# Second MLP of an attention and two-MLP kernel: weight sums and low parts on VectorE, tied to later steps

## The chip, the cores and the metric

The kernel runs on one core of a Trainium2 chip. The metric is device time in microseconds (us) of one execution; the kernel before takes 1208.81 us, the median of three executions (1207.57 to 1208.98).

## The reference, cut to what matters

Windowed attention (4 batches, 8 heads, 768 positions, head size 64) gives x with 3072 tokens of 512 features. A first MLP makes y = (sigmoid(x Wg) * (x Wv)) Wo with 1536 hidden features. The second MLP, the stage of the change, is

```
h = y @ w_in                                  # 3072 x 512 times 512 x 2048
g = h * (1.0 / (1.0 + np.exp(-1.702 * h)))
out = g @ w_out                               # 2048 x 512
```

The weights come as 64-bit floats. Every product is computed in three matmuls on split operands: a high part (h) in the type fp32r and a low part (l), the rest of the value, as h*h + h*l + l*h.

## The kernel before, in words

All work is added as tasks to a list (`add`), each with an engine, an estimated duration, the keys that it reads and writes, and perhaps a due time. `Schedule.run` walks through time by these estimates: on each engine it starts the ready task with the earliest due time, and it never leaves an engine idle for a later, more urgent task. The order it finds is the order of the instructions on each engine's queue; on the chip each engine works its queue off in that order and waits where an operand is late. Products on TensorE get due times from a running clock (`clock`, advanced by `c_mm`), and all that feeds them gets due times from theirs.

The 3072 tokens are six blocks of 512. The second MLP takes blocks 0 and 1 plainly: 16 steps per block, f = 0 to 15, each `first_product` (12 matmuls: 8 "high", line 742, and 4 "low", line 749), then sigmoid on ScalarE (766), the multiplication on VectorE (769, tile sig), the high part on ScalarE (772, tile gh) and the low part (776, tile gl), then `gemm4` (12 matmuls, 720) for the step before, whose result stays in four banks over 16 steps. The low part of block 0 is made by GpSimd (POOL), that of block 1 by VectorE.

Blocks 2 and 3, and then 4 and 5, are taken as two pairs. For a pair the first product is done in a form with 7 products instead of 8 (m1 to m7 in `part_product`, line 1248, 6 matmuls each) on sums of quarter blocks. This needs two preparations.

- `combine(j)`, j = 0 to 7, forms sums of the weights of two slots: `whole` adds high and low part of a slot (1093, tiles cw_a and cw_b, on POOL), `sums` forms four combinations (1103 to 1106, tile cw_s, one task of four VectorE instructions), `high` (1109, ScalarE, tile cw_h) and two `low` (1113, VectorE, tile cw_l), and DMAs of SP store all to wc_dram. The tiles exist once, so one combine follows another. `fetch` loads the parts back into a ring (sb_r).
- `x_prep(b)` loads eight tiles of the blocks' y (1203), forms eight differences (1209, VectorE) and cuts fourteen operands into high (1188, ScalarE) and low part (1192; eight of the fourteen on POOL, six on VectorE).

All eight combines and the first x_prep are ready as soon as the weights are converted, in block 0. Within a pair, each j has the seven products of a group, gating on ScalarE and VectorE (1260, 1264, 1289, 1292, 1275, 1278), and one or two `gemm4` of hidden parts made earlier (`fill`). After j = 7 come 16 rounds of one `gemm4` and one `halves` (the high and low part of a stored g, 1275 and 1278); only then, in the order of the program, the second pair begins. The x_prep of the second pair stands ahead of these rounds; its loads depend on y alone.

Of the kernel before, what the change touches and what calls it, by code (L numbers as in the profile page):

```python
# [8 lines left out]
F32 = mybir.dt.float32  # L9
# [6 lines left out]
ALU = mybir.AluOpType  # L16
AX = mybir.AxisListType

P = 128
# [100 lines left out]
def c_dve(n, k=1):  # L120
    return k * 0.13 + n / 960.0
# [6 lines left out]
def c_pool(n):  # L128
    return 0.1 + n * 2.4e-3
# [3 lines left out]
def kernel(  # L133
# [14 lines left out]
    nc = tc.nc  # L148
# [7 lines left out]
    F2 = w2_in.shape[1] // P  # L156
# [7 lines left out]
    BLK = 512  # L164
# [8 lines left out]
    add = sch.add  # L173
# [540 lines left out]
    def mm3(ps_out, lhs, rhs, first, last):  # L714

        n = len(lhs)
        for i in range(n):
            (lh, ll), (rh, rl) = lhs[i], rhs[i]
            for j, (a, c) in enumerate(((lh, rh), (lh, rl), (ll, rh))):
# [5 lines left out]
                    stop=(last and i == n - 1 and j == 2),  # L725
                )

    def c_mm(n, k):
        return k * (n / 2400.0 + 0.0025)

    def product(dur, fn, r, w, load=1.0):
        add("pe", dur, fn, r=r, w=w, due=clock[0])
        clock[0] += dur * load
# [81 lines left out]
    for i in range(4):  # L815
        x = Bufs(pro, "", [], main)
# [177 lines left out]

    freed = []
    for f in range(F1):
        freed.append((3 * f + 1, f))
# [12 lines left out]
        convert(slot_in2[f], cols(w2_in, f))  # L1012
        convert(slot_out2[f], rows(w2_out, f))

    def gemm4(f, i, banks, row, end=False, after=()):

        gh, gl = ghs[i], gls[i]
        s = slot_out2[f]

        def fn():  # L1020
            w = slots[s]
            for tt in range(TT):
                c = slice(tt * P, (tt + 1) * P)
                mm3(bank[banks[tt]], [(gh[:, c], gl[:, c])], [(w[:, 0, :], w[:, 1, :])], f == 0, f == F2 - 1)

        product(
            c_mm(512, 3 * TT),
            fn,
            [("w", s, 0), ("w", s, 1), ("gh", i), ("gl", i), *after],
            [("bank", k) for k in banks],  # L1030
        )
        if f < F2 - 1:
            return
        for tt in range(TT):
            st, kst = (fts[tt], ("f", tt)) if end else stage()
            bk = banks[tt]
            h = 256 if end and tt == TT - 1 else 512
            for c in range(0, 512, h):

                def ev(on_dve, c=slice(c, c + h), st=st, bk=bk):  # L1040
                    if on_dve:
                        nc.vector.tensor_copy(st[:, c], bank[bk][:, c])
                    else:
                        nc.scalar.activation(st[:, c], bank[bk][:, c], AF.Copy)

                def store(tt=tt, c=slice(c, c + h), st=st):
                    r = row + tt * P
                    nc.sync.dma_start(out=out[r : r + P, c], in_=st[:, c])

                on_dve = bool(tt % 2) or c > 0  # L1050
                k = (kst, c) if h < 512 else kst
                add("dve" if on_dve else "act", c_dve(h), lambda ev=ev, d=on_dve: ev(d), r=[("bank", bk)], w=[k])
                add("sp", 0.45, store, r=[k], nbytes=P * h * 4)
# [33 lines left out]
    def combine(j):  # L1087
        s0, s1 = slot_in2[2 * j], slot_in2[2 * j + 1]

        def whole(x, s):  # L1090
            def fn():
                w = slots[s]
                nc.gpsimd.tensor_tensor(out=cw[x], in0=w[:, 0, :].bitcast(F32), in1=w[:, 1, :].bitcast(F32), op=ALU.add)

            add("pool", c_pool(512), fn, r=[("w", s, 0), ("w", s, 1)], w=["c" + x])

        whole("wa", s0)
        whole("wb", s1)

        def sums():  # L1100
            wa, wb, s = cw["wa"], cw["wb"], cw["s"]
            tt = nc.vector.tensor_tensor
            tt(out=s[:, 0, :], in0=wb[:, :H2], in1=wb[:, H2:], op=ALU.add)  # L1103
            tt(out=s[:, 2, :], in0=wa[:, :H2], in1=wb[:, :H2], op=ALU.subtract)  # L1104
            tt(out=s[:, 1, :], in0=s[:, 0, :], in1=wa[:, :H2], op=ALU.subtract)
            tt(out=s[:, 3, :], in0=wa[:, H2:], in1=s[:, 1, :], op=ALU.subtract)

        def high():
            nc.scalar.activation(cw["h"], cw["s"], AF.Copy)  # L1109

        def low(h):
            c = slice(2 * h, 2 * h + 2)
            nc.vector.tensor_tensor(  # L1113
                out=cw["l"][:, c, :], in0=cw["s"][:, c, :], in1=cw["h"][:, c, :].bitcast(F32), op=ALU.subtract
            )

        add("dve", c_dve(4 * H2, 4), sums, r=["cwa", "cwb"], w=["cws"])
        add("act", c_act(4 * H2), high, r=["cws"], w=["cwh"])
        for h in range(2):
            add("dve", c_dve(2 * H2), lambda h=h: low(h), r=["cws", "cwh"], w=["cwl"])  # L1120

        def put(m, n, part, src, keys):
            def fn():
                at = wc_dram[j * NMP + m : j * NMP + m + n]
                if part is None:
                    nc.sync.dma_start(out=at[0].rearrange("p (h k) -> p h k", h=2), in_=src())
                else:
                    nc.sync.dma_start(out=at[:, :, part * H2 : (part + 1) * H2].rearrange("c p k -> p c k"), in_=src())

            kw = [("wc", j, m + i, h) for i in range(n) for h in ((0, 1) if part is None else (part,))]  # L1130
            add("sp", 0.45, fn, r=keys, w=kw, nbytes=n * P * H2 * (8 if part is None else 4))

        for m, s, c in ((MA11, s0, 0), (MA12, s0, H2), (MA22, s1, H2)):
            put(m, 1, None, lambda s=s, c=c: slots[s][:, :, c : c + H2].bitcast(F32), [("w", s, 0), ("w", s, 1)])
        put(MS1, 4, 0, lambda: cw["h"].bitcast(F32), ["cwh"])
        put(MS1, 4, 1, lambda: cw["l"].bitcast(F32), ["cwl"])

    for j in range(NPR):
        combine(j)

    xt, ringh, gbs, work, ys = {}, {}, {}, {}, {}
    NRH = 14
# [51 lines left out]
        add("act", c_act(BLK), hi, r=[kst], w=[("X", m, k)])  # L1194
        add("pool" if pool else "dve", c_pool(BLK) if pool else c_dve(BLK), lo, r=[kst], w=[("X", m, k)])

    def x_prep(b):
        for k in range(2):
            tk = 4 + k
            for i, (m, bb) in enumerate(((k, b), (k, b + 1), (2 + k, b), (2 + k, b + 1))):  # L1200

                def load(i=i, m=m, bb=bb):
                    nc.sync.dma_start(out=ys[i], in_=y_dram[m * P : (m + 1) * P, bb * BLK : (bb + 1) * BLK])

                add("sp", 0.45, load, r=[("y", m, bb)], w=[KYS[i]], nbytes=P * BLK * 4)

            def sub(o, x, y):
                def fn():
                    nc.vector.tensor_tensor(out=ys[o], in0=ys[x], in1=ys[y], op=ALU.subtract)

                add("dve", c_dve(BLK), fn, r=[KYS[x], KYS[y]], w=[KYS[o]])

            def cut(m, i, pool):
                split_x(m, k, lambda: ys[i], KYS[i], pool)

            cut(XB11, 0, True)
            sub(tk, 1, 0)
            cut(XT1, tk, False)
            cut(XB21, 2, True)
            sub(tk, 3, tk)  # L1220
            cut(XT2, tk, False)
            cut(XB22, 3, True)
            sub(1, 3, 1)
            cut(XT3, 1, True)
            sub(tk, 2, tk)
            cut(XT4, tk, False)

# [8 lines left out]
            kr = [("wc", g % NPR, STEPS[m][0], x) for x in range(2)]  # L1236
            add("sp", 0.45, fn, r=kr, w=[("ring", h)], nbytes=P * 512 * 4)

    def part_product(g, m, bk, first):
        h = (g * NMP + SEQ.index(m)) % NRH  # L1240
        x = STEPS[m][1]

        def fn():
            w = ringh[h]
            for k in range(2):
                for wl, xl in ((0, 0), (0, 1), (1, 0)):
                    o = wl * H2 + k * P
                    nc.tensor.matmul(  # L1248
                        bank[bk],
                        w[:, o : o + P],  # L1250
                        xt[x, k][:, xl, :],
                        start=first and k == 0 and wl == 0 and xl == 0,
                        stop=k == 1 and wl == 1,
                        skip_group_check=not first,
                    )

        product(c_mm(512, 6), fn, [("ring", h)] + xkey(x), [("bank", bk)])

    def snap(n, bk):
        add("act", c_act(BLK), lambda: nc.scalar.activation(work[n], bank[bk], AF.Copy), r=[("bank", bk)], w=[n])  # L1260
# [23 lines left out]
    def gate2(src, ksrc, f=None):  # L1284
# [11 lines left out]
            return halves(lambda: sigs[i], ks)  # L1296
        add("dve", c_dve(BLK), mul, r=[ksrc, ks], w=[("gB", f)])

    pend = None
    nh = 0  # L1300
    for b in range(NBP):
        xb = (NB + b) % 2
        for f in range(F2):
            hb = Hb[nh % 2]
            nh += 1
            first_product(slot_in2[f], xb, BLK, hb)
            i, tail = gated(BLK, hb, 1.702, hb, b == 0)
            tail()
            if pend:
                gemm4(*pend)  # L1310
            if f == 0 and b + 1 < NBP:
                y_in(b + 1, (xb + 1) % 2)
            pend = (f, i, O[b], b * BLK)
# [5 lines left out]
    homes = [(m, k) for m in (XB21, XT2, XB22, XT3, XT4) for k in range(2)]  # L1319
    for (m, k), s in zip(homes, rest2 + slot_in2):  # L1320
        open_slot_as(s, f"sb_x{m}{k}", F32R, x_one(m, k), [("X", m, k)])
    x_prep(NBP)
    left = slot_in2[len(homes) - len(rest2) :]
    for i in range(NRH // 2):

# [18 lines left out]
    for sb in range(NSB):  # L1344
# [5 lines left out]
        for j in range(NPR):  # L1350
# [18 lines left out]
            gate2(lambda: work["s5"], "s5", 2 * j + 1)  # L1369
            if fill:  # L1370
                gemm4(*fill.pop(0))
            part_product(g, "m4", a, False)
            ic = gate2(lambda a=a: bank[a], ("bank", a))
            if g + 2 < NSB * NPR:
                fetch(g + 2)
            fill += [(2 * j, ia, oa, row), (2 * j + 1, ic, oa, row)]
        if sb + 1 < NSB:
            x_prep(NBP + 2 * sb + 2)
        end = sb == NSB - 1
        for f in range(F2):  # L1380
            gemm4(*fill.pop(0))
# [36 lines left out]
```

## Time and profile before

| What | Value |
|---|---|
| Median of three executions | 1208.81 us |
| The profiled execution | 1209.48 us, of which the span from first to last instruction is 1207.7 us |
| PE (TensorE matmul) busy | 1180.2 us, 98% of the span, 7352 instructions |
| DVE (VectorE) busy | 712.2 us, 59% |
| ACT (ScalarE) busy | 522.2 us, 43% |
| POOL (GpSimd) busy | 153.3 us, 13% |
| Chain of waits that ended last | 90% PE, 5% DVE, 2% ACT |

Matmuls overlap in the pipeline: a busy time of 390 ns per matmul is not its cost. The cost is the distance from the start of one matmul to the start of the next. In a row, "x4" merges four instructions, the time in front is the first one's start, and a bracket tells how long the engine stood idle before the row and what released it.

### The profile page before, as it was taken

The numbers are of one execution on the slowest core, as the hardware profiler recorded it, in microseconds if no ns is written. First come the engines' busy times: TensorE is split into PE (matmuls) and PEld (weight loads), VectorE is DVE, ScalarE is ACT, GpSimd is POOL, SyncE is SP. The second block draws the span as 40 slices with busy tenths as digits, with TensorE's granted clock in tenths as the row PEclk, the third lists the DMA queues.
The fourth block names the chain that finished last, engine by engine and source line by source line (L and its number), as shares of the span: only waits on it lengthen the run. The fifth ranks groups of instructions, "written<-read, shape, count | busy, mean of one in ns | idle before, by whom it ended". The sixth has DMA issues, their size and how long they took to land.

```text
span 1207.7 us, 19184 instructions
## 1 busy us (share of the span) xinstructions
PE 1180.2 (98%) x7352; PEld 982.2 (81%) x7352; DVE 712.2 (59%) x1406; ACT 522.2 (43%) x847; POOL 153.3 (13%) x128
## 2 busy tenths in 40 slices
PE   6799999999999999999999999999999999999998
PEld 5688799988888888888888877888888878888887
DVE  6898848884588438816778776252143374143342
ACT  4598743443344223413577643342243343243332
POOL 2221210000010000000211276320000030000000
PEclk9799999999999999999999999999999999999999
DMA  9556333233123202400477654032144443234100
GB/s 217 141 176 199 115 81 54 50 53 76 31 50 63 50 13 50 97 2 19 130 257 243 197 198 158 31 103 94 55 148 123 123 139 95 63 114 122 44 36 35
DMA packets 200780, 122.08 MB, mean 101 GB/s; under 512 B 138608, under 2 KB 173680, under 8 KB 200688
## 3 DMA queue, kind: packets, MB, share of 16 engines
q1 hardware_dynamic: 197232, 114.56, 35.0%
q10 hardware_dynamic: 3456, 6.29, 1.4%
q8 instruction: 58, 0.95, 0.3%
q14 instruction: 34, 0.28, 0.1%
HBM read 93.54 MB, written 27.26 MB: 100 GB/s over the span
## 4 chain that ended last, share of the span: by engine, by line
PE 90%; DVE 5%; ACT 2%; issue 1%; DMA 1%; POOL 0%; DVEq 0%; SPq 0%; ACTq 0%; POOLq 0%
PE bank L742 25%; PE bank L720 19%; PE bank L917 16%; PE bank L749 12%; PE bank L1248 12%; PE bank L656 2%; PE bank L506 2%; DVE cw_l L1113 1%; DVE cw_s L1103 1%; PE bank L596 1%; ACT cw_h L1109 0%; DVE pw L574 0%; PE bank L397 0%; DVE cw_s L1104 0%; PE bank L389 0%
## 5 line engine op out<-in xcount | busy, mean ns | idle before, releaser
L742 PE MATMUL bank<-xh,w 128*128 128x512 f32 (+1 forms) x784 | 284.7, 370 | 3.5 <-ACT w L286 1.6
L742 PE MATMUL bank<-xl,w 128*128 128x512 f32 (+1 forms) x784 | 282.9, 368 | 0.0
L720 PE MATMUL bank<-w,gh 128*128 128x512 f32 x768 | 237.7, 391 | 0.1
L749 PE MATMUL bank<-xh,w 128*128 128x512 f32 (+1 forms) x784 | 191.7, 370 | 0.0
L742 PEld LDWEIGHTS bank<-xh,w 128*128 128x128 f32 x784 | 148.0, 189 | 31.6 <-DVE sig L769 2.8
L720 PEld LDWEIGHTS bank<-w,gh 128*128 128x128 f32 x768 | 144.5, 188 | 30.7 <-ACT gh L1275 0.6
L742 PEld LDWEIGHTS bank<-xl,w 128*128 128x128 f32 x784 | 147.9, 189 | 24.2
L769 DVE TENSOR_TENSOR sig<-bank,sig 128x512 f32<-128x512 f32 (+1 forms) x114 | 73.1, 641 | 154.9 <-PE bank L749 80.2
L749 PEld LDWEIGHTS bank<-xh,w 128*128 128x128 f32 x784 | 138.0, 188 | 24.9
L917 PE MATMUL bank<-gh,w 128*128 128x512 f32 (+1 forms) x656 | 158.2, 364 | 0.0
L720 PE MATMUL bank<-w,gl 128*128 128x512 f32 x384 | 150.3, 392 | 3.8 <-POOL gl L776 2.2
L917 PEld LDWEIGHTS bank<-gh,w 128*128 128x128 f32 x656 | 114.4, 189 | 19.7
L772 ACT ACTIVATE gh<-sig 128x512 fp32r<-128x512 f32 (+1 forms) x114 | 67.4, 592 | 138.2 <-DVE sig L769 121.9
L766 ACT ACTIVATE sig<-bank 128x512 f32<-128x512 f32 (+1 forms) x114 | 63.9, 560 | 139.5 <-PE bank L749 130.7
L1248 PE MATMUL bank<-sb_x,sb_r 128*128 128x512 f32 x480 | 115.8, 389 | 0.5 <-ACT sb_s L1260 0.5
L1248 PEld LDWEIGHTS bank<-sb_x,sb_r 128*128 128x128 f32 x480 | 90.0, 188 | 19.6 <-ACT sb_s L1260 0.9
L720 PEld LDWEIGHTS bank<-w,gl 128*128 128x128 f32 x384 | 72.3, 188 | 20.1 <-POOL gl L776 2.7
L776 DVE TENSOR_TENSOR gl<-sig,gh 128x512 fp32r<-128x512 f32 (+1 forms) x98 | 64.9, 662 | 37.2 <-ACT gh L772 26.6
L631 DVE STREAM_TRANSPOSE pt<-raw 32x256 f32<-32x256 f32 x184 | 80.1, 435 | 2.8
L917 PE MATMUL bank<-gl,w 128*128 128x512 f32 (+1 forms) x328 | 80.5, 367 | 0.0
L574 POOL TENSOR_TENSOR raw<-e,sm 96x448 f32<-96x448 f32 x23 | 23.2, 1009 | 405.8 <-DVE sm L566 405.8
L1264 DVE TENSOR_TENSOR sb_s<-bank,sb_s 128x512 f32<-128x512 f32 x48 | 33.1, 691 | 62.4 <-PE bank L1248 54.3
(127 smaller groups left out, 1350.8 us busy)
## 6 DMA issues: line engine op xcount, KB each, us to landing
sb_r<-wc_dram SPq DMA_DIRECT2D x112, 256.0 KB
raw<-in_moe_w_out_dram SPq DMA_DIRECT2D x24, 512.0 KB
raw<-in_moe_w_in_dram SPq DMA_DIRECT2D x16, 512.0 KB
y_dram<-f ACTq DMA_DIRECT2D x24, 256.0 KB
wc_dram<-w SPq DMA_DIRECT2D x24, 256.0 KB
out_dram<-f SPq DMA_DIRECT2D x23, 256.0 KB
vn<-in_v_dram SPq DMA_DIRECT2D x24, 240.0 KB
f<-in_q_dram SPq DMA_DIRECT2D x276, 16.0 KB
```

The costliest lines, as they stand in the source:

```text
L506: nc.tensor.matmul(bk[c * CH : (c + 1) * CH, p * KW : (p + 1) * KW], T["qt"][r, p, c * CH : (c + 1) * CH], T["kt"][r, p, c, :], start=True ...
L631: nc.vector.transpose(T["pt"][r * CH : (r + 1) * CH, :, c * CH : (c + 1) * CH], T["pn"][c * CH : (c + 1) * CH, :, kb * CH : (kb + 1) * CH],)
L720: nc.tensor.matmul(ps_out, a, c, start=(first and i == 0 and j == 0), stop=(last and i == n - 1 and j == 2),)
L742: nc.tensor.matmul(bank[bk][:, :n], w[:, 0, ts[t]], x[xb][:, t, c0 : c0 + n], start=t == 0 and x is xhs, stop=False)
L749: nc.tensor.matmul(bank[bk][:, :n], w[:, 1, ts[t]], xhs[xb][:, t, c0 : c0 + n], start=False, stop=t == NK - 1)
L766: nc.scalar.activation(sig[:, :n], bank[src_sig][:, :n], AF.Sigmoid, scale=scale)
L769: nc.vector.tensor_tensor(out=sig[:, :n], in0=bank[src_val][:, :n], in1=sig[:, :n], op=ALU.mult)
L772: nc.scalar.activation(gh[:, :n], sig[:, :n], AF.Copy)
L776: eng.tensor_tensor(out=gl[:, :n], in0=sig[:, :n], in1=gh[:, :n].bitcast(F32), op=ALU.subtract)
L917: nc.tensor.matmul(bank[Y[m]][:, c0 : c0 + n], w[:, wi, m * P : (m + 1) * P], g[:, :n], start=f == 0 and j == 0 and c0 == 0, stop=f == F1 ...
L1248: nc.tensor.matmul(bank[bk], w[:, o : o + P], xt[x, k][:, xl, :], start=first and k == 0 and wl == 0 and xl == 0, stop=k == 1 and wl == 1, ...
L1264: nc.vector.tensor_tensor(out=work[n], in0=bank[bk], in1=work[n], op=ALU.add)
```

## The change

- `whole` and the low parts of block 0 and of x_prep move from POOL to VectorE. POOL keeps the four low parts of `y_in` in block 0 (963) and its share of the weight conversion.
- `combine(j)` is no longer ready at once. The `gemm4` that runs in step 6 + 2j of the 32 steps of blocks 0 and 1 writes a mark ("cm", j), and the two `whole` of combine j read it.
- The loads of the first x_prep read the mark of combine 7 (step 20), those of the second x_prep the mark ("p2", sb) that the last product m4 (j = 7) of the first pair writes.
- From the second MLP on, the planner's cost of a matmul of 512 columns is 512/2400 us + 32/2400 us = 0.2267 us in place of 0.2158 us. This constant enters no instruction, only the order.

```diff
+    step_ns = [0.0025]
+
     def c_mm(n, k):
-        return k * (n / 2400.0 + 0.0025)
+        return k * (n / 2400.0 + step_ns[0])
...
+    step_ns[0] = 32 / 2400.0
     freed = []
...
-    def gemm4(f, i, banks, row, end=False, after=()):
+    def gemm4(f, i, banks, row, end=False, mark=None):
...
-            [("w", s, 0), ("w", s, 1), ("gh", i), ("gl", i), *after],
-            [("bank", k) for k in banks],
+            [("w", s, 0), ("w", s, 1), ("gh", i), ("gl", i)],
+            [("bank", k) for k in banks] + ([mark] if mark else []),
...
         def whole(x, s):
             def fn():
                 w = slots[s]
-                nc.gpsimd.tensor_tensor(out=cw[x], in0=w[:, 0, :].bitcast(F32), in1=w[:, 1, :].bitcast(F32), op=ALU.add)
-
-            add("pool", c_pool(512), fn, r=[("w", s, 0), ("w", s, 1)], w=["c" + x])
+                nc.vector.tensor_tensor(out=cw[x], in0=w[:, 0, :].bitcast(F32), in1=w[:, 1, :].bitcast(F32), op=ALU.add)
+
+            add("dve", c_dve(512), fn, r=[("w", s, 0), ("w", s, 1), ("cm", j)], w=["c" + x])
...
-
-    for j in range(NPR):
-        combine(j)
...
-    def x_prep(b):
+    def x_prep(b, mark):
...
-                add("sp", 0.45, load, r=[("y", m, bb)], w=[KYS[i]], nbytes=P * BLK * 4)
+                add("sp", 0.45, load, r=[("y", m, bb), mark], w=[KYS[i]], nbytes=P * BLK * 4)
...
-            cut(XB11, 0, True)
+            cut(XB11, 0, False)
...
-            cut(XB21, 2, True)
+            cut(XB21, 2, False)
...
-            cut(XB22, 3, True)
+            cut(XB22, 3, False)
...
-            cut(XT3, 1, True)
+            cut(XT3, 1, False)
...
-    def part_product(g, m, bk, first):
+    def part_product(g, m, bk, first, mark=None):
...
-        product(c_mm(512, 6), fn, [("ring", h)] + xkey(x), [("bank", bk)])
+        product(c_mm(512, 6), fn, [("ring", h)] + xkey(x), [("bank", bk)] + ([mark] if mark else []))
...
+    CW0 = 6
...
-            i, tail = gated(BLK, hb, 1.702, hb, b == 0)
+            i, tail = gated(BLK, hb, 1.702, hb, False)
             tail()
+            j, odd = divmod(b * F2 + f - CW0, 2)
+            now = not odd and 0 <= j < NPR
             if pend:
-                gemm4(*pend)
+                gemm4(*pend, mark=("cm", j) if now else None)
+            if now:
+                combine(j)
...
-    x_prep(NBP)
+    x_prep(NBP, ("cm", NPR - 1))
...
-            part_product(g, "m4", a, False)
+            part_product(g, "m4", a, False, ("p2", sb) if j == NPR - 1 else None)
...
-            x_prep(NBP + 2 * sb + 2)
+            x_prep(NBP + 2 * sb + 2, ("p2", sb))
```

## Rows read from the trace of the kernel before

**Rows 1.** Busy us (and instructions) of each engine by stretch; granted clock PEclk.

```profile
700.00:800.00 100.00, 96.56 (x416) 78.72 (x415) 54.26 (x71) 37.86 (x61) 55.57 (x39) 0.98 0.40 133
800.00:900.00 100.00, 100.00 (x443) 82.80 (x442) 37.54 (x56) 30.45 (x52) 1.31 (x1) 1.00 0.31 98
```

**Rows 2.** PE alone: stretch, its length, busy us (x matmuls), PEclk, DMA.

```profile
689.94:1203.90 513.96, 508.19 (x2225) 1.00 0.32 98
1154.70:1203.90 49.20, 49.11 (x217) 1.00 0.07 27
```

**Rows 3.** PE in order of time, blocks 0 and 1: start, us, instruction, idle before.

```profile
705.39 0.50 PE L742 MATMUL bank<-xh,w 128*128 128x512 f32 x1 [0.78 <-DVE sig L769]
...
738.85 0.50 PE L742 MATMUL bank<-xh,w 128*128 128x512 f32 x1 [0.43 <-DVE sig L769]
...
744.45 0.61 PE L720 MATMUL bank<-w,gh 128*128 128x512 f32 x2
...
747.30 0.50 PE L720 MATMUL bank<-w,gl 128*128 128x512 f32 x1 [2.23 <-POOL gl L776]
...
753.13 0.62 PE L720 MATMUL bank<-w,gh 128*128 128x512 f32 x2
```

**Rows 4.** Five engines and PEld, the stretch behind the longest wait.

```profile
747.00:752.00 5.00, 4.70 (x14) 3.75 (x15) 3.52 (x7) 1.58 (x2) 1.80 (x2) 0.66 0.56 189
```

**Rows 5.** All engines in order of time, ahead of that wait.

```profile
743.50 0.61 ACT L772 ACTIVATE gh<-sig 128x512 fp32r<-128x512 f32 x1
...
743.85 1.73 POOL L1093 TENSOR_TENSOR cw_b<-w 128x512 f32<-128x512 f32 x1
...
745.54 1.71 POOL L776 TENSOR_TENSOR gl<-sig,gh 128x512 fp32r<-128x512 f32 x1
```

**Rows 6.** PE in order of time, first pair to second, and later.

```profile
987.97 0.61 PE L720 MATMUL bank<-w,gh 128*128 128x512 f32 x2
989.35 0.50 PE L720 MATMUL bank<-w,gl 128*128 128x512 f32 x1 [0.76 <-DVE gl L1278]
...
992.06 0.74 PE L720 MATMUL bank<-w,gh 128*128 128x512 f32 x2
993.64 0.50 PE L720 MATMUL bank<-w,gl 128*128 128x512 f32 x1 [0.84 <-DVE gl L1278]
...
1059.28 3.04 PE L1248 MATMUL bank<-sb_x,sb_r 128*128 128x512 f32 x12 [0.52 <-ACT sb_s L1260]
```

**Rows 7.** All engines in order of time, ahead of the wait at 989.

```profile
986.41 1.74 POOL L1192 TENSOR_TENSOR sb_x<-f,sb_x 128x512 fp32r<-128x512 f32 x1
...
986.92 1.78 DVE L1209 TENSOR_TENSOR sb_y<-sb_y,sb_y 128x512 f32<-128x512 f32 x1
...
988.62 0.68 DVE L1278 TENSOR_TENSOR gl<-sig,gh 128x512 fp32r<-128x512 f32 x1
```

**Rows 8.** DVE by line and shape, 689 to 752: count, busy us, mean ns, idle.

```profile
L1113 DVE TENSOR_TENSOR cw_l<-cw_s,cw_h 128x512 fp32r<-128x512 f32 x16 | 17.5, 1122 | 6.3 <-ACT cw_h L1109 4.3 <-DMA wc_dram<-cw_l 2.0
L1103 DVE TENSOR_TENSOR cw_s<-cw_b 128x256 f32<-128x256 f32 x8 | 8.8, 1096 | 4.3 <-POOL cw_b L1093 4.3
...
L1105 DVE TENSOR_TENSOR cw_s<-cw_s,cw_a 128x256 f32<-128x256 f32 x8 | 3.3, 414 | 0.0
```

**Rows 9.** All engines in order of time, one step of block 1.

```profile
821.15 1.07 PE L749 MATMUL bank<-xh,w 128*128 128x512 f32 x4
...
822.31 0.60 ACT L766 ACTIVATE sig<-bank 128x512 f32<-128x512 f32 x1 [5.59 <-PE bank L749]
...
824.33 0.69 DVE L776 TENSOR_TENSOR gl<-sig,gh 128x512 fp32r<-128x512 f32 x1 [0.70 <-ACT gh L772]
...
827.04 0.39 PE L720 MATMUL bank<-w,gl 128*128 128x512 f32 x1
```

**Rows 10.** PE alone, blocks 0 and 1, between two waits.

```profile
707.30:737.30 30.00, 30.00 (x133) 1.00 0.56 187
```

**Rows 11.** DVE in order of time, one gemm4 round behind the second pair.

```profile
1163.49 0.69 DVE L1278 TENSOR_TENSOR gl<-sb_g,gh 128x512 fp32r<-128x512 f32 x1 [2.03 <-ACT gh L1275]
```

## The prediction, made before the changed kernel ran

> **What bounds the kernel now.** I read the table by stretch first. From 700 us on TensorE is never idle for long, yet it starts 416 matmuls between 700 and 800 us and 443 in the next 100 us [rows 1]: 27 fewer is some 6 us lost where blocks 0 and 1 run, and there POOL is busy for 55.6 us against 1.3. Second, the unhindered price of a matmul: behind the second pair 217 matmuls, one of them begun before, stand in 49.2 us [rows 2]; start to start that is 0.2267 us.
>
> Third, the ceiling. From 689.94 to 1203.90 us there are 2225 matmuls [rows 2], the first of them begun before. At 0.2267 us each they fill 504.4 us; the stretch is 514.0 us. So **9.6 us** are lost to waits in the whole second MLP, and nothing on the list can give more. The last store behind it and the time around the span (1209.48 less 1207.7) stay. The Trainium skill (TensorE: Matmul & The Clock Gate, Part 1) gives 215.7 ns for 512 columns back to back, and by it 34 us would be lost in this stretch. No stretch read here runs at that, so the measurement decides.
>
> Fourth, where the 9.6 us lie: the rows of TensorE with an idle bracket, each with the engine that released it.
> - (a) 705.39: 0.78 us behind the multiplication on VectorE; 738.85: 0.43 us behind another [rows 3].
> - (b) 744.45 to 747.30: two matmuls are 0.45 us, so 2.40 us are lost, behind gl on POOL. From 747.30 to 753.13 come 18 matmuls, 4.08 us of work in 5.83: another 1.75 us [rows 3]. In that stretch the granted clock is 0.66 on the mean, so part of it ran at 1.2 instead of 2.4 GHz behind the idle time [rows 4]. Together **4.15 us**.
> - (c) 987.97 to 989.35: 0.93 us; 989.35 to 992.06, ten matmuls: 0.44 us; 992.06 to 993.64: 1.13 us [rows 6]. Together **2.5 us**, at the passage from the first pair to the second.
> - (d) 1059.28: 0.52 us behind ScalarE [rows 6].
> Sum 8.4 us; the other 1.2 us are slower matmuls right behind the gaps and spread.
>
> **The change, part by part.**
>
> **Combine.** What stood ahead of (b)? gh was ready at 744.11; its low part began on POOL at 745.54, since POOL was at cw_b until 745.58, and ended at 747.25 [rows 5]. Both, whole and low part, leave POOL, and no combine is ready there any more. On VectorE a low part takes 0.69 us [rows 9], so gl ends at about 744.9, when TensorE wants it: (b) goes, and the 0.43 us of (a), which lie among combines too. The 0.78 us stay for the most part: that multiplication follows a first product that ended only just before, and the order of those products is not edited. I take back **4.5 us** (4.15 and 0.43, rounded down).
>
> What comes in their place? The combines then stand in steps 6 to 21, one in two steps, that is one in 48 matmuls or 10.9 us. Work on VectorE per combine: two whole of 0.69, four sums of 0.41 [rows 8], two low of 0.69: 4.4 us. Gating takes two times 1.38 us. That is 7.2 of 10.9 us. ScalarE gets no more than before. Does a step bear it? In a clean step the low matmuls start at 821.15, four of them; sigmoid begins at 822.31 and gl ends at 825.02; the first matmul that wants gl starts at 827.04 [rows 9]: 2.0 us of slack. VectorE's queue runs in order: behind a whole or a sums task stand the multiplication and gl of the step, and for them TensorE. One sums task is 1.65 us, under the slack; sums ahead of the multiplication and a low ahead of gl are 2.3 us, 0.3 over. A whole that is ordered ahead of its mark's gemm4 holds the queue for up to 2.7 us, 0.7 over. Bounds of the cost: 0, and at eight combines with 0.3 and 0.7 each 8 us. The nearest row is that of TensorE between the waits, where eight combines stood in 63 us [rows 8], one in 8 us and not in 11, and 133 matmuls fill 30.0 us, at 0.2267 us nothing lost [rows 10]. I take **0.5 us**.
>
> The two instructions of SP that store cw_h and cw_l move with each combine; the fetches that read the last of them belong to j = 7, more than 60 us later, behind step 31. The slots that combine reads are opened anew only behind it, in steps from 16 on.
>
> VectorE's durations were judged as follows. The sums on line 1105 take 414 ns, those of the same shape on 1103 take 1096 ns on the mean, and the low parts 1122 ns against 690 [rows 8, 9]; the long ones lie beside a POOL instruction, as 1.78 us at 986.92 beside 1.74 us at 986.41 [rows 7]. The Trainium skill (SBUF — State Buffer, Who interferes with whom) says why: a VectorE instruction with two inputs in SBUF and a GpSimd instruction that reads SBUF take one shared port in turn, for a whole instruction. By that rule the excess goes with POOL's work. If the long durations came of something else, a combine would be four instructions of 1.12 us and sums of 1.10 and three times 0.41, 6.8 us instead of 4.4, and with the gates (two multiplications of 0.69, two gl of 1.12) 10.4 of 10.9 us: no room, which is the first rival below.
>
> **Low parts of block 0.** 16 on POOL go, 16 of 0.69 us come on VectorE, one per step; they are in the 1.38 us above. Block 1 has done so and shows the slack of rows 9. Four low parts of y_in stay on POOL; beside one, gl may take 1.1 us longer (1.78 less 0.69), under the slack. Zero; 0.5 us if that cover fails at all.
>
> **The first x_prep.** Eight loads wait on SP for step 20's gemm4. Fourteen low parts and eight differences, 22 × 0.69 = 15.2 us, run on VectorE beside gates that leave 4.1 of 5.4 us: 20 us behind their loads. The first pair begins behind step 31, 11 steps or 60 us later. Behind the loads SP has fetches and stores of finished tokens. Zero, with 30 us of cover.
>
> **The second x_prep.** At 988.62 gl of the last j was late behind a difference held by POOL [rows 7], the second gap likewise [rows 6]. The eight loads now wait on SP for the last m4, so the differences and cuts come only behind that group's gating. Behind the loads stand fetches of the ring, not needed before the second pair. The work then lies beside 16 rounds of gemm4, 43.5 us: 15.2 us and 16 low parts, 11 us, on VectorE. In a round gh and gl have some slack: VectorE idles for 2.03 us ahead of gl [rows 11]. A difference on VectorE (0.69) and a high part on ScalarE (0.61 [rows 5]) in the way are 1.3 us, under that. So 2.5 us go and I take 0.3 for what comes: **2.2 us**. Bounds: all 2.5, and a loss (the second rival).
>
> **The planner's constant** agrees with the trace now. It moves the order of all later work; (d) and the 0.78 us may go, or one like them come: from +1.3 to −1.3 us, taken as 0.
>
> **Sum:** 4.5 − 0.5 + 2.2 = 6.2 us, and 0.6 us of slower matmuls behind the gaps: 6.8 us. 1209.48 − 6.8 = 1202.7 us for the profiled execution. The median is 0.67 us lower, 1208.81 − 6.8 = **1202.0 us**.
>
> **The rivals.**
> 1. Combine crowds the gates on VectorE (18 in 100). Each combine brings one wait of 0.6 to 1 us in its steps: 8 × 0.8 = 6.4 us in place of the 0.5 us taken, and nearly all that is won is given back: 1208.8 − 6.8 + 5.9 = 1207.9 us. For it: VectorE has 7.2 of 10.9 us, in queue order. Against: rows 10.
> 2. **Slower** (9 in 100): in the 16 rounds there is nothing else to run, since the second pair's operands come later than now. If x_prep's 22 instructions on VectorE and 14 on ScalarE make gl late in 14 of the 16 gemm4 by the 0.83 us that a wait at (c) costs on the mean, that is 11.6 us; with (c) gone and 4.0 us won at the combines: 1208.8 + 11.6 − 2.5 − 4.0 = 1213.9 us. It decides from eight such waits on. Against: 1.3 us in the way under 2.0 us.
> 3. The change does not do what it says to the path (8 in 100): the re-planned order puts other waits where these were, as 0.78 and 0.52 have no combine or x_prep behind them. 1207.5 to 1209.5 us.
>
> **Chances.** My forecast 65 in 100 (1199.5 to 1204.5: all 9.3 us gone, or 4.3). This measurement can tell 0.2% or 2.4 us from no change: faster is below 1206.4. Rival 1 puts half of its 18 there (waits of 0.6 us), the other half within the bound; rival 3 lies within it, rival 2 above it. Faster 0.74, same 0.17, slower 0.09. The range takes in the ceiling, 1199.2, and the better half of rival 1: 1199.2 to 1207.5.
>
> **What would show it.** Right: POOL without work in blocks 0 and 1 save four low parts; sums of 0.41 us throughout; no row of TensorE released by POOL; 443 matmuls in each 100 us from 710 on; no gap between the last m4 of the first pair and the next m1. Wrong: brackets "DVE sig" or "DVE gl" every 11 us between 730 and 820 (rival 1), a row of them in the 43 us behind m4 (rival 2), or gaps whose sum is still 9 us elsewhere (rival 3).

## The result, and the profile after

The changed kernel takes **1198.74 us**, median of four runs (1198.03 to 1200.05), against 1208.89 us (1207.57 to 1209.60) for the kernel before: a ratio of 0.9919 (0.9901 to 0.9936). It gained 10.15 us where 6.8 were forecast, and ended 0.46 us under the range. The profiled execution took 1200.05 us, of which the span is 1198.3. From the first edit to the end of combine the code moved by two or three lines: the multiplication is now L771, its high part L774, gl L778, `whole` L1096, the sums L1106 to L1109, cw_h L1112, the low parts of combine L1116. From x_prep on the numbers are those of the kernel before.

First the same view as [rows 1], over four stretches (PE, PEld, DVE, ACT, POOL busy; PEclk; DMA):

```profile
700.00:800.00 100.00, 100.00 (x443) 82.84 (x442) 52.66 (x93) 32.61 (x51) 5.14 (x4) 1.00 0.29 97
800.00:900.00 100.00, 100.00 (x443) 82.84 (x442) 48.10 (x76) 37.80 (x64) 0.00 (x0) 1.00 0.42 130
900.00:1000.00 100.00, 100.00 (x443) 82.81 (x442) 49.82 (x78) 42.66 (x73) 0.00 (x0) 1.00 0.48 138
1000.00:1100.00 100.00, 100.00 (x442) 82.82 (x442) 41.19 (x62) 33.35 (x56) 0.00 (x0) 1.00 0.34 100
```

443 matmuls in 700 to 800 us where [rows 1] have 416, and 443 or 442 in each stretch after it: the rate that the prediction called unhindered is now held throughout. POOL has 5.14 us left, the four low parts of `y_in`; the last:

```profile
716.77 1.30 POOL L965 TENSOR_TENSOR xl<-f,xh 128x512 fp32r<-128x512 f32 x1 [1.24 <-ACT xh L962]
```

TensorE alone over the same 2225 matmuls as the first of [rows 2] (the second MLP and the last 17 of the first), and its first and last row:

```profile
690.18:1194.50 504.32, 504.31 (x2225) 1.00 0.33 100
```

```profile
690.18 0.39 PE L744 MATMUL bank<-xh,w 128*128 128x512 f32 x1
...
1194.11 0.39 PE L720 MATMUL bank<-w,gl 128*128 128x512 f32 x1
```

From start to start that is 503.93 us, or 2223 times 0.2267. In the kernel before the last matmul started at 1203.43: 513.48 us. The difference is 9.55 us, the whole ceiling of the prediction, and no row of TensorE behind 690 us has a bracket any more. The profiled executions differ by 9.43 us; the medians by 10.15, and the 0.7 between them is within the 2 us over which the runs of each kernel spread. That spread lies ahead of the stretch, as far as traces tell: the kernels of experiments 2 and 12 take the same 503.93 us for it and began it at 688.54 and 687.81 us, in executions of 1198.41 and 1197.70 us.

VectorE by line and shape, 689 to 830 us, against [rows 8]: low parts 688 ns (1122 before), sums 422 (1096), gl 690.

```profile
L778 DVE TENSOR_TENSOR gl<-sig,gh 128x512 fp32r<-128x512 f32 x25 | 17.3, 690 | 18.5 <-ACT gh L774 18.3
L1116 DVE TENSOR_TENSOR cw_l<-cw_s,cw_h 128x512 fp32r<-128x512 f32 x16 | 10.8, 688 | 3.0 <-ACT cw_h L1112 3.0
...
L1106 DVE TENSOR_TENSOR cw_s<-cw_b 128x256 f32<-128x256 f32 x8 | 3.4, 422 | 0.2
```

Most telling is what stands where the 0.78 us at 705.39 were [rows 3]. TensorE and then ScalarE, the kernel after:

```profile
702.87 1.98 PE L751 MATMUL bank<-xh,w 128*128 128x512 f32 x8
704.69 0.62 PE L720 MATMUL bank<-w,gh 128*128 128x512 f32 x2
...
707.41 0.39 PE L744 MATMUL bank<-xh,w 128*128 128x512 f32 x1
```

```profile
701.83 0.60 ACT L939 ACTIVATE f<-bank 128x512 f32<-128x512 f32 x1 [0.62 <-DMA y_dram<-f]
...
702.88 0.60 ACT L939 ACTIVATE f<-bank 128x512 f32<-128x512 f32 x1 [0.46 <-ACT f L939]
```

And ScalarE of the kernel before, at the same place:

```profile
704.77 1.06 ACT L1109 ACTIVATE cw_h<-cw_s 128x1024 fp32r<-128x1024 f32 x1 [0.36 <-DVE cw_s L1106]
705.73 1.07 ACT L937 ACTIVATE f<-bank 128x512 f32<-128x512 f32 x2
```

Before, the last evictions of the first MLP stood behind a combine's cw_h and the next high product was queued first, where it waited for its multiplication. After, no combine is there, the evictions are done three microseconds earlier, and the `gemm4` runs in the gap: twelve matmuls of cover where there were none. The order of those products did change, though no edit names it. The kernel of experiment 3, whose combines are ready as early as before but run on VectorE, has no wait at this place either: its `gemm4` starts at 704.19. So the place of the combines is one way to that order and not the only one.

### The profile page after: what moved, and what is told of

It is laid out like the page before. It is cut to its first block, busy times and chain, and to the rows that moved or that the text cites. A ratio compares the mean times of both kernels' runs of the same rounds, so it can differ in the third digit from the quotient of the medians.

```text
span 1198.3 us, 19147 instructions
## 1 busy us (share of the span) xinstructions
PE 1176.4 (98%) x7352; PEld 981.9 (82%) x7352; DVE 717.3 (60%) x1454; ACT 522.2 (44%) x847; POOL 81.9 (7%) x80
## 4 chain that ended last, share of the span: by engine, by line
PE 94%; DVE 2%; SPq 1%; DMA 1%; issue 1%; ACT 0%; DVEq 0%; POOL 0%; POOLq 0%
PE bank L744 25%; PE bank L720 22%; PE bank L919 16%; PE bank L751 13%; PE bank L1248 13%; PE bank L656 2%; PE bank L506 2%; SPq L311 1%; PE bank L596 1%; DMA qkn_a<-in_mem_k_dram 0%; DVE pw L574 0%; PE bank L397 0%; PE bank L389 0%; DMA qn<-in_q_dram 0%; DVE sm L563 0%
## 5 line engine op out<-in xcount | busy, mean ns | idle before, releaser
L771 DVE TENSOR_TENSOR sig<-bank,sig 128x512 f32<-128x512 f32 (+1 forms) x114 | 73.1, 641 | 136.6 <-PE bank L751 77.4
L774 ACT ACTIVATE gh<-sig 128x512 fp32r<-128x512 f32 (+1 forms) x114 | 67.5, 592 | 141.6 <-DVE sig L771 119.4
L778 DVE TENSOR_TENSOR gl<-sig,gh 128x512 fp32r<-128x512 f32 (+1 forms) x114 | 74.1, 650 | 49.3 <-ACT gh L774 38.6
L919 PEld LDWEIGHTS bank<-gl,w 128*128 128x128 f32 x328 | 56.8, 189 | 9.8
```

The source lines that it names most:

```text
L771: nc.vector.tensor_tensor(out=sig[:, :n], in0=bank[src_val][:, :n], in1=sig[:, :n], op=ALU.mult)
L774: nc.scalar.activation(gh[:, :n], sig[:, :n], AF.Copy)
L778: eng.tensor_tensor(out=gl[:, :n], in0=sig[:, :n], in1=gh[:, :n].bitcast(F32), op=ALU.subtract)
L919: nc.tensor.matmul(bank[Y[m]][:, c0 : c0 + n], w[:, wi, m * P : (m + 1) * P], g[:, :n], start=f == 0 and j == 0 and c0 == 0, stop=f == F1 ...
```

## The experiments

Two theories. **Engine:** POOL's work is the cause of the gaps in blocks 0 and 1 (gl waits behind cw_b on POOL, VectorE's instructions are long beside it); taking it away is the gain, and the ties and the planner's constant are worth little. **Order** (the rival): the eight combines, ready all at once, stand in front of the gates in every queue; tying them to steps is the gain, on whichever engine they run. For x_prep likewise: cuts on VectorE against loads that are held. Times are medians; intervals are those of the ratio to the kernel before, timed on the same chip. "Before plus" and "after less" say which kernel was edited.

**1. The constant alone** (before plus):

```diff
+    step_ns[0] = 32 / 2400.0
```

> The kernel before with the planner's new matmul cost alone; all work stays where it was. My theory (the waits came of POOL's share and of work standing in the way): only the waits that have no combine and no x_prep behind them, 0.78 us at 705 and 0.52 us at 1059, can go, and the long wait on POOL near 747 and the waits on gl near 989 stay in some place: 1207.6 to 1209. Rival (a planner that knows TensorE's real pace is what closes the gaps): 1199 to 1201, and TensorE waits for nothing behind 690 us.

Measured: 1212.92 us, ratio 1.0039 (1.0025 to 1.0053), slower. Both theories missed. Three of TensorE's eight waits, in order of time:

```profile
702.42 0.76 PE L744 MATMUL bank<-xh,w 128*128 128x512 f32 x1 [2.39 <-DVE sig L771]
...
723.26 0.50 PE L744 MATMUL bank<-xh,w 128*128 128x512 f32 x1 [0.83 <-DVE sig L771]
...
731.57 0.50 PE L744 MATMUL bank<-xh,w 128*128 128x512 f32 x1 [1.62 <-DVE sig L771]
```

A truer cost of a matmul gave a worse order: on VectorE the multiplication at 701.68 now stood behind two low parts of 2.51 us together and four sums of 0.41 us. All of it is combine work that was ready too early.

**2. All but the constant** (after less):

```diff
-    step_ns[0] = 32 / 2400.0
```

> The changed kernel with the old matmul cost in the planner. My theory: 1198.7 to 1200.0, at most the 0.78 and 0.52 us come back. Rival (the constant closes the gaps): 1205 or more, with waits on VectorE in the steps that hold combines.

1198.76 us, 0.9920 (0.9903 to 0.9937), no wait of TensorE, again 503.93 us. The constant gives nothing here; with the combines tied it does no harm either.

**3. Combines on VectorE, not tied** (after less):

```diff
-r=[("w", s, 0), ("w", s, 1), ("cm", j)]
+r=[("w", s, 0), ("w", s, 1)]
```

> The changed kernel, but whole no longer reads the mark, so all eight combines are ready at the end of the first MLP; they stay on VectorE. My theory (POOL was the cause): VectorE takes a combine into each 6 us, gates go first, and waits are 0 to 1.5 us in all: 1198.7 to 1200.2. Rival (the ties to later steps closed the gap near 747): some 4 us of waits between 700 and 750 come back, 1202.5 to 1203.5.

1203.04 us, 0.9956 (0.9939 to 0.9973): 4.3 us of the gain are gone although POOL has nothing more to do than in the kernel after. This contradicts the engine theory. VectorE, with one row of POOL, then TensorE:

```profile
719.90 1.73 POOL L965 TENSOR_TENSOR xl<-f,xh 128x512 fp32r<-128x512 f32 x1 [0.57 <-ACT xh L962]
...
720.39 1.78 DVE L1096 TENSOR_TENSOR cw_b<-w 128x512 f32<-128x512 f32 x1
...
722.10 1.28 DVE L1116 TENSOR_TENSOR cw_l<-cw_s,cw_h 128x512 fp32r<-128x512 f32 x2
723.30 0.41 DVE L1106 TENSOR_TENSOR cw_s<-cw_b 128x256 f32<-128x256 f32 x1
...
724.95 0.69 DVE L1096 TENSOR_TENSOR cw_a<-w 128x512 f32<-128x512 f32 x1
725.56 0.68 DVE L771 TENSOR_TENSOR sig<-bank,sig 128x512 f32<-128x512 f32 x1
```

```profile
726.96 0.73 PE L720 MATMUL bank<-w,gh 128*128 128x512 f32 x2 [1.75 <-ACT gh L774]
...
728.10 0.51 PE L720 MATMUL bank<-w,gl 128*128 128x512 f32 x1 [0.41 <-DVE gl L778]
```

The sigmoid had ended at 721.37; its multiplication began at 725.56, behind parts of two combines. The bracket names ScalarE (gh), but the lateness is VectorE's queue: read one step further back. POOL has a share in it still: one `whole` lay beside a low part of `y_in` and took 1.78 us and not 0.69, some 1.1 of the 4.2 us. By estimate the 3.1 us left would still be over the 2.0 us of slack.

**4. Tied, but on POOL** (after less: `whole` and the low parts of block 0 go back):

```diff
-nc.vector.tensor_tensor(out=cw[x], ...)  add("dve", ...)
+nc.gpsimd.tensor_tensor(out=cw[x], ...)  add("pool", ...)
-            i, tail = gated(BLK, hb, 1.702, hb, False)
+            i, tail = gated(BLK, hb, 1.702, hb, b == 0)
```

> The changed kernel with whole and the low parts of block 0 on POOL again, ties kept. My theory (POOL's queue and its hold on VectorE were the cause): two whole of 1.3 us ahead of a low part of 1.3 us put gl up to 1 us beyond the 2.0 us of slack at the five combines that lie in block 0, and sums and low parts on VectorE are 1.1 us and more again where POOL works: 1201 to 1204. Rival (the ties alone suffice): no wait of TensorE on POOL, 1198.7 to 1199.5.

1198.99 us, 0.9924 (0.9905 to 0.9943), no wait of TensorE. The mirror of 3: POOL works and VectorE's instructions are long beside it, and nothing is lost (504.07 us of TensorE's stretch against 503.93). VectorE by line, 689 to 830 us, then POOL:

```profile
L1116 DVE TENSOR_TENSOR cw_l<-cw_s,cw_h 128x512 fp32r<-128x512 f32 x16 | 14.9, 949 | 7.4 <-ACT cw_h L1112 7.4
L1109 DVE TENSOR_TENSOR cw_s<-cw_a,cw_s 128x256 f32<-128x256 f32 x8 | 8.3, 1035 | 0.3
```

```profile
L778 POOL TENSOR_TENSOR gl<-sig,gh 128x512 fp32r<-128x512 f32 x16 | 21.1, 1318 | 50.0 <-ACT gh L774 36.1 <-issue 13.9
```

**5. Loads of the second x_prep not held** (after less):

```diff
-r=[("y", m, bb), mark]
+r=[("y", m, bb)] + ([mark] if mark[0] == "cm" else [])
```

> The changed kernel, but the loads of the second x_prep no longer read the mark of the last m4; its cuts stay on VectorE. My theory (at the passage both the place of the work and POOL made gl late): differences and cuts stand among the gates of j = 7 again, each 0.69 us and not 1.7, so of the 2.5 us of waits near 989 between 0 and 1.2 come back: 1198.7 to 1200.0. Rival (holding the loads is what closed that gap): 2 us or more come back, 1200.7 to 1201.5.

1200.30 us, 0.9935 (0.9923 to 0.9948). TensorE loses 1.4 us of its stretch (503.93 to 505.30), with two waits, of which one is the 0.52 us of [rows 6]:

```profile
984.32 0.50 PE L720 MATMUL bank<-w,gl 128*128 128x512 f32 x1 [0.24 <-DVE gl L1278]
...
1049.96 3.03 PE L1248 MATMUL bank<-sb_x,sb_r 128*128 128x512 f32 x12 [0.52 <-ACT sb_s L1260]
```

**6. Eight cuts of each x_prep back on POOL** (after less; 7 undoes the holding of 5 as well):

```diff
-            cut(XB11, 0, False)
+            cut(XB11, 0, True)
...
```

> The changed kernel with eight cuts of each x_prep on POOL again, loads held. My theory: the work lies beside the 16 rounds of gemm4, and a gl that POOL holds up by 1.1 us stays under the slack of 2.0 us: 1198.7 to 1199.3, one or two short waits at most. Rival (POOL alone made the gap): 1200.5 to 1201.5, with TensorE waiting for gl behind a POOL instruction.

1211.09 us (1206.74 to 1212.73), 1.0019 (1.0009 to 1.0029): slower than the kernel before, which has the same cuts on POOL. Both theories missed by about ten. One edit left out turns the gain into a loss. Where, 10 and 11 tell. In the profiled execution TensorE's 2225 matmuls take 513.17 us, 9.24 more than in the kernel after: 5.9 us are waits, the rest slower matmuls. That execution is the lowest of the twelve. The mean granted clock falls as their times rise, from 0.992 in it to 0.989 in the two highest; what else these lost is not shown.

**7. Cuts on POOL and loads not held.**

> The changed kernel with both edits of x_prep undone for the second pair: loads not held, eight cuts on POOL. Both theories: the 2.5 us of waits at the passage come back, 1201.0 to 1201.7. If it stays under 1200, neither edit of x_prep mattered, and combines or the planner's constant closed that gap.

1208.22 us, 1.0001 (0.9992 to 1.0009), expected near 1201. TensorE's stretch is 8.97 us longer than in the kernel after, with four waits from 820 to 838 us and three from 984 to 990. Experiments 6 and 7 missed for one reason: I had reckoned with the second x_prep alone and put the first, with its 30 us of cover, at nothing. In 6 the price of the second was too low besides, as 11 shows.

**8. The ties alone** (before plus marks of the eight combines; all on POOL as before, old constant):

```diff
+r=[("w", s, 0), ("w", s, 1), ("cm", j)]
...
+            if now:
+                combine(j)
```

> The kernel before with the ties of the combines alone: whole, the low parts of block 0 and eight cuts per x_prep on POOL, no loads held, old matmul cost. Theory now (the ties end the waits in block 0, but they push the first x_prep behind combine 7, where cuts on POOL cost as much): waits of 3 to 5 us between 810 and 840, the 2.5 and 0.5 us at the passage stay, none from 700 to 760: 1205.5 to 1209.5. Rival (the ties are worth 4 to 5 us by themselves, whatever x_prep does): 1203.5 to 1204.8.

1204.55 us, 0.9970 (0.9960 to 0.9981), the rival's time. No wait of TensorE between 690 and 829 us, so (a) and (b) are gone, 5.36 us; (c) and (d) stay, and new ones come between:

```profile
829.67 0.50 PE L744 MATMUL bank<-xh,w 128*128 128x512 f32 x1 [0.76 <-DVE sig L771]
...
841.78 0.73 PE L720 MATMUL bank<-w,gh 128*128 128x512 f32 x2 [0.48 <-ACT gh L774]
```

5.36 less 1.24 is 4.1 us; TensorE's stretch gives 4.0 (513.48 to 509.45), the medians 3.5. The first and the last of the eight POOL cuts of the first x_prep, in the kernel before and then here:

```profile
763.51 1.29 POOL L1192 TENSOR_TENSOR sb_x<-sb_y,sb_x 128x512 fp32r<-128x512 f32 x1
...
806.64 1.31 POOL L1192 TENSOR_TENSOR sb_x<-f,sb_x 128x512 fp32r<-128x512 f32 x1 [6.86 <-ACT sb_x L1188]
```

```profile
820.72 1.30 POOL L1191 TENSOR_TENSOR xh_sb<-f,xh_sb 128x512 fp32r<-128x512 f32 x1 [21.86 <-ACT xh_sb L1187]
...
836.06 1.74 POOL L1191 TENSOR_TENSOR sb_x<-f,sb_x 128x512 fp32r<-128x512 f32 x1
```

Eight cuts in 43 us have become eight in 15. By the code, x_prep's tiles lie where weight slots and the combine's own tiles lay (four of its y tiles where cw_h and cw_l were), so it can't begin before the last combine is done; tied combines end late, and x_prep becomes a burst, though its own loads are not held here. No run parts this from the order that the planner found.

**9. The cuts alone** (before plus: all cuts on VectorE).

> The kernel before with all cuts of both x_preps on VectorE, nothing else. Theory now: the waits from 700 to 750 (4.2 to 5.3 us) stay, since the combines are as before; of the 2.5 us at the passage half or more goes, as where the loads were not held: 1206.5 to 1208.3. Rival (the cuts on POOL are the cause of all): 1203 or less.

1205.07 us, 0.9981 (0.9971 to 0.9990). The waits at the passage are all gone, the others stay:

```profile
704.54 0.50 PE L742 MATMUL bank<-xh,w 128*128 128x512 f32 x1 [0.70 <-DVE sig L769]
...
746.46 0.50 PE L720 MATMUL bank<-w,gl 128*128 128x512 f32 x1 [2.21 <-POOL gl L776]
```

So the cuts take (c) without the held loads: 2.3 us by the ratio, 2.5 in the prediction.

**10 and 11. Cuts on POOL for the first x_prep only, and for the second only** (after less):

```diff
+            cut(XB11, 0, b == NBP)     # 10
+            cut(XB11, 0, b > NBP)      # 11
...
```

> The changed kernel with the cuts of the first x_prep alone on POOL. Theory (both x_preps share the loss of the kernel with all cuts on POOL): the waits from 818 to 838 come back, 3.5 to 5 us, and none at the passage: 1202 to 1204.5. Rival (the second x_prep alone carries that loss): under 1200.

> The changed kernel with the cuts of the second x_prep alone on POOL, loads held. Theory: the waits near 993 to 996 come back with the slower matmuls behind them, 3 to 7 us, and none before 840: 1201.5 to 1206. Rival (the slack of the gemm4 rounds hides them, as I predicted): 1198.5 to 1199.5.

10: 1203.64 us, 0.9965 (0.9952 to 0.9977). 11: 1203.85 us, 0.9961 (0.9948 to 0.9974). Each costs some 5 us (TensorE's stretch is 5.68 and 4.64 us longer than in the kernel after), and each waits at its own place only. In 10, TensorE and then its stretch with the granted clock:

```profile
824.83 0.50 PE L720 MATMUL bank<-w,gl 128*128 128x512 f32 x1 [0.83 <-DVE gl L778]
...
833.91 0.73 PE L720 MATMUL bank<-w,gh 128*128 128x512 f32 x2 [1.50 <-ACT gh L774]
835.47 0.50 PE L720 MATMUL bank<-w,gl 128*128 128x512 f32 x1 [0.83 <-DVE gl L778]
```

```profile
835.00:840.00 5.00, 4.53 (x13) 0.66 0.44 160
```

In 11, all engines in order of time, with the wait that follows:

```profile
986.02 1.68 DVE L1209 TENSOR_TENSOR f<-sb_y,f 128x512 f32<-128x512 f32 x1
...
987.62 1.78 DVE L1192 TENSOR_TENSOR xl_sb<-sb_y,xl_sb 128x512 fp32r<-128x512 f32 x1
...
990.51 1.71 POOL L1192 TENSOR_TENSOR sb_x<-f,sb_x 128x512 fp32r<-128x512 f32 x1
991.02 1.75 DVE L1278 TENSOR_TENSOR gl<-sb_g,gh 128x512 fp32r<-128x512 f32 x1
...
992.82 0.50 PE L720 MATMUL bank<-w,gl 128*128 128x512 f32 x1 [2.69 <-DVE gl L1278]
```

A gl that takes 0.68 us alone takes 1.75, and the instructions ahead of it in VectorE's queue 1.68 and 1.78: together more than the 2.0 us of slack. In the kernel after, every instruction of these bursts takes 0.68 or 0.69 us:

```profile
989.11 0.68 DVE L1278 TENSOR_TENSOR gl<-sb_g,gh 128x512 fp32r<-128x512 f32 x1
...
991.52 0.68 DVE L1278 TENSOR_TENSOR gl<-sb_g,gh 128x512 fp32r<-128x512 f32 x1
```

**12. Three edits** (before plus ties, held loads and cuts on VectorE; `whole` and the low parts of block 0 stay on POOL, the constant is the old one; the lines are those of 8, 5 and 9).

> The kernel before with three of the edits: combines tied, loads of both x_preps held, all cuts on VectorE. Whole and the low parts of block 0 stay on POOL and the planner's matmul cost stays as it was. Theory (these three are all that it takes): TensorE waits for nothing behind 690 us, 1198.0 to 1199.6. Rival (the moves of whole and low parts or the constant are needed once both are missing): 1201 or more.

1197.70 us, 0.9922 (0.9910 to 0.9935): the whole gain, equal to the kernel after. The answer to [rows 1]:

```profile
700.00:800.00 100.00, 100.00 (x442) 82.78 (x442) 41.19 (x66) 32.64 (x51) 47.99 (x35) 1.00 0.28 95
```

POOL is busy for 48 of 100 us and TensorE loses nothing: POOL's share in [rows 1] was a companion of the gap, not its cause. Whether the first x_prep's loads must be held besides was not tried by itself.

## Why the prediction was wrong

The ceiling held: 9.6 us, found by counting matmuls, were to be had, and 9.55 were had. The place list (a) to (d) held as well. Wrong was what would stay.

- **The step that failed** is the sum's remainder. It left 2.8 us behind: the 0.78 us that "stay for the most part", 0.5 us for crowding by combine, 0.3 us for what the second x_prep brings, the 0.52 us of (d) under "the constant, taken as 0", and 0.6 of the 1.2 us of slow matmuls. All measured zero: TensorE has no wait left, and its matmuls run at 0.2267 us throughout. The 0.78 was the one with a wrong reason: "the order of those products is not edited". The planner orders all that follows from all that precedes it; with the combines away from step 0, ScalarE's evictions came earlier and a `gemm4` stood in front of the product that waited (so too in experiment 8, which has the ties alone).
- **Combine, 4.5 us:** the size was near (5.36 us gone), the cause was not. I credited it to both operations leaving POOL, with the ties as a companion. Experiments 3, 4 and 8 give it to the ties: without them 4.3 us are lost on VectorE too; with them POOL may keep the work.
- **Crowding, 0.5 us, the first rival:** with one combine in two steps VectorE is busy for 52.66 of 100 us and no gate is late. Untied, the rival's mechanism is real: it is experiment 3.
- **Low parts of block 0: zero, right** (experiment 4).
- **First x_prep: zero, right for the kernel as changed, and too easily.** The 30 us of cover hold for its own deadline. They don't cover the gates of block 1 that share its queue: with the cuts on POOL it costs 5.7 us (experiment 10).
- **Second x_prep, +2.2 us:** (c) went in full, 2.5. But I gave it to the held loads and the cuts together. The cuts on VectorE do it alone (experiment 9), and the held loads take another 1.4 us, (d) and a wait of 0.24 us at the passage among it (experiment 5): in all six kernels whose loads were free (before, 1, 5, 7, 8, 9) the wait for sb_s of 0.5 us stands behind 1040 us, in every kernel with held loads it is absent. How a load before the passage makes sb_s late 60 us on, through the planned order, was not followed.
- **The constant, taken as 0:** zero in the kernel after, 3.9 us of loss on the kernel before. Its bounds of 1.3 us were too narrow, since they came from two waits and not from what a new order may do.
- **The second rival** (gemm4 rounds starve VectorE's gl) did not come, but its mechanism is what 11 shows, at POOL's prices. Its 0.83 us per wait was (c) divided by three, though (c) has two waits.
- **The range** ended at the ceiling, 1199.2, worked from the profiled execution, with nothing for the spread of medians. TensorE's stretch shows that no more than the ceiling was won, so the 0.46 us under the range are put down to that spread.

The Trainium skill's rule on two inputs in SBUF (SBUF — State Buffer, Who interferes with whom) was used to judge the long instructions, and the runs bear it out: 0.68 us alone, 1.75 beside POOL (experiment 11). The same section of the Trainium skill says that a VectorE instruction with at most one input in SBUF, outside the modes that use two ports, is spared. The trace agrees: the multiplication, whose other input is a bank, keeps 0.68 us in the kernel before while `whole` runs on POOL.

```profile
737.60 1.73 POOL L1093 TENSOR_TENSOR cw_b<-w 128x512 f32<-128x512 f32 x1
738.12 0.68 DVE L769 TENSOR_TENSOR sig<-bank,sig 128x512 f32<-128x512 f32 x1
```

Whether the excess costs anything is a matter of place: in 4 nothing, in 10 and 11 five microseconds.

The time ahead of 690 us was not studied: the stretch begins 0.2 us later than in the kernel before, and between 686.53 and 690.18 us over all the traces. What moves it stays open.

## What to carry to other kernels

Count the bound engine's instructions against its unhindered step: the ceiling came out right to 0.1 us, and work that is tied to the step that can bear it may take all of it, so a range should pass the ceiling by the spread of the runs. Work that is ready early and needed late should be given a place: a queue in planned order puts it in front of urgent work on any engine. It isn't all: for the combines the place was enough, on either engine (experiments 3, 4); for the cuts, which came in a burst, the engine mattered (6, 9, 10, 11). Edits of an order are not additive: take each out alone and put each in alone before you credit it.

## What the runs showed of the hardware

- Behind some waits TensorE's granted clock fell: to 0.66 right behind 2.23 us [rows 3, 4], to 0.66 behind 1.50 and 0.83 us within two (experiment 10), to 0.75 from 995 to 1000 us, 2 us after a wait of 2.69 us had ended (experiment 11; 0.66 in the 5 us right behind it): part of each at 1.2 GHz instead of 2.4. So these waits cost more than their brackets: 5.68 us for 3.16 in 10, 4.64 us for 2.69 in 11. The length of a wait doesn't settle it. After the 1.75 us of experiment 3 the clock stayed at 1.00, which is 2.4 GHz, and so it did in experiment 6 from 835 to 840 us, behind waits of 1.49 and 0.83 us like those of 10. What does settle it no run here shows. TensorE in 11, then in 3:

```profile
995.00:1000.00 5.00, 5.00 (x18) 0.75 0.59 181
```

```profile
725.00:730.00 5.00, 2.85 (x11) 1.00 0.57 193
730.00:735.00 5.00, 4.46 (x20) 1.00 0.55 182
```

- Side by side, a VectorE and a POOL instruction of 128x512 both grow: gl from 0.68 (the kernel after) to 1.75 us (experiment 11), POOL's cut from 1.30 (experiment 8) to 1.71 (11). The price reached the time where both queues were dense (experiments 8, 10, 11, and the kernel before at 987 us [rows 7]), and not where POOL's cuts were spread over 43 us (the kernel before, 763 to 808 us) or its work was tied to steps (4, 12).
